# Edge rows prepared once a matrix, measured durations in the planner, and a row that goes into the queries by DMA

## The chip, the cores and the metric

The kernel runs on one core of a Trainium2 chip. The metric is device microseconds of one execution; lower is better. An engine is named as in the profile: PE (TensorE, matmul), PEld (its weight loads), ACT (ScalarE), DVE (VectorE), POOL (GpSimd) and SP (SyncE, which here issues every DMA).

## The reference

Two independent computations on 2048 x 448 inputs, whose results stand side by side in the output.

```python
# A: Fourier mixing, real part of a DFT over the hidden and the sequence axis
a = einsum("bsd,ed->bse", x, dft_hid_re); b = einsum("bsd,ed->bse", x, dft_hid_im)
y = einsum("ts,bse->bte", dft_seq_re, a) - einsum("ts,bse->bte", dft_seq_im, b)
# B: full softmax attention, 16 heads of 28
qkv = x @ wqkv                       # split into q, k, v
p = softmax(q @ k.T * 28 ** -0.5)
out = (p @ v).reshape(S, D) @ wo
return concatenate([y, out], axis=-1)
```

All is float32. The inputs of B are scaled up by 8, so the scores are large and the softmax needs a shift close to each row's maximum.

## The kernel before, in words

Products are made more exact by splitting a value into a rounded part and its rest ("hi" and "lo", type fp32r) and adding two or three matmuls. Tiles are 128 rows; a chunk of queries is 512 columns, four chunks to a head.

**Attention (B).** Projections of q, k and v come first and go to DRAM. For each head, `first_tiles` takes the first 128 keys against all four chunks of queries (L1096), copies the scores to `kept` (ACT, L1100), and makes a shift for each query from the maxima over these keys: DVE transposes each chunk into the buffer `mb` (L1101), reduces it (L1102), joins the partitions (L1108 to L1113), and spreads the shift out again by a transpose into `mb` (L1122). Row 96 of that buffer is copied into row 96 of the query tile `q` (L1125, on DVE or POOL, one partition of 512 elements), and the whole buffer is added to the kept scores (L1127), which then go through the exponential (L1129). With the shift in `q`, the other fifteen key tiles get it inside the matmul: scores L1155 (60 a head), exponential straight from the PSUM bank L1161, and four matmuls with v for each key tile, L1138. So no L1155 of a chunk can start before that chunk's row is in `q`. There is one `mb` buffer, used in turn.

**Fourier mixing (A).** The hidden DFT (`hidden`, L900) makes `u`; the sequence DFT (`sequence`, L985) multiplies it with the 2048 x 2048 matrices. Since these matrices are symmetric, only half of them is multiplied; the kernel folds and compares the other parts (`mirrored`): for each of 8 row tiles `tt`, two halves `g` and two matrices (`part`) it loads four blocks into `wraw` (8 places), folds them (L654, L672), takes the largest leftover difference (L645) and keeps the edge columns (L659, L662). Rows that have no mirror image, 0 and 1024 of each matrix, are multiplied on their own: in the first half `g == 0` of each tile the folded row is taken from `wraw`, split into hi and lo in a small tile `ext` at partitions 0, 32 and 64 (L677 to L679), its source is set to zero (L681), and in the second half a 65-row matmul multiplies `ext` with `peaks` (the short L985). The maxima (L645) of that block wait for L681. `acc`, a sum kept on DVE (L921), is used by one late matmul, L1253.

**The order.** Nothing is scheduled at run time. `Schedule.run` is a planner in the program's own Python: each task has the engines that may do it with a cost in us for each, a due key, tasks it waits for and buffers it needs. It plays the engines forward; whichever engine comes free takes the task with the lowest key that is ready, and tasks are written out in that order, each engine's queue being in order on the chip. A task that names both POOL and DVE goes to the one that comes free first in the plan. SP's DMAs have a modelled flow and at most 8 in flight. So the costs decide which engine does what and in which order, though not how long it takes. PE takes scores, PV matmuls and the "fill" (projections, both DFTs), whose order among themselves is fixed. `kept` has 16 places and holds exponentials, staging and outputs. `big` holds x in its split form during the projections and later `u`, which leaves its tail free.

Of the kernel before, what the change touches and what calls it, by code (L numbers as in the profile page):

```python
# [11 lines left out]
F32 = mybir.dt.float32  # L12
# [12 lines left out]
P = 128  # L25
# [43 lines left out]
def f32(ap):  # L69
    return ap.bitcast(F32)  # L70
# [280 lines left out]
def tile_kernel(ctx, tc, xa, wre, wim, wd, xb, wqkv, wo, out):  # L351
# [33 lines left out]
    x_raw, x_hl = new("xraw", [P, NH, 4], F32), new("xhl", [P, 2, NH, 4], F32R)  # L385
    ext_s, peaks = new("ext", [P, P], F32R, 2), new("peak", [P, 2, E], F32R)
    w_hi, w_lo = new("whi", [P, 3, 4, P], F32R), new("wlo", [P, 3, 4, P], F32R)
# [5 lines left out]
    kept_s = new("kept", [P, 2, CH], F32, NKEPT)  # L393
    mb_s = new("mb", [P, CH], F32, 1, True)
    sm_s = new("sm", [P, 2, NT], F32, 2)
# [178 lines left out]
    class Piece:  # L574


        def __init__(self, src, key, kind="c", early=False, home=None, after=(), wide=False):
            self.hi, self.lo = whi.slot(), wlo.slot()
            raw = self.raw = home or wraw.slot()
            ld = self.ld = dma(key, lambda: nc.sync.dma_start(raw.t, src()), deps=after, acq=[raw])  # L580
            if kind == "c":
                a = sch.add({"POOL": 1.0, "ACT": ACT_S} if wide else {"POOL": 1.0}, key + 1, lambda g: eng_copy(g, self.hi.t, raw.t),
                            deps=[ld], acq=[self.hi], use=[raw])
            else:
                a = act(key + (0 if early else 1), lambda: nc.scalar.activation(self.hi.t, raw.t, AF.Copy), ACT_S, soon=SOON,  # L585
                        deps=[ld], acq=[self.hi], use=[raw])
            at = key + (0 if early else 1.5)
            both = ("DVE",) if early else ("POOL", "DVE") if wide else ("POOL",)
            e = {g: {"DVE": 0.8, "POOL": 1.25}[g] for g in both}
            n = 4 if kind == "c" else 3  # L590
            b = sch.add(e, at, lambda g: eng[g].tensor_tensor(  # L591
                self.lo.t[:, :n], raw.t[:, :n], f32(self.hi.t)[:, :n], op=ALU.subtract),
                deps=[a], acq=[self.lo], use=[raw, self.hi])
            self.ready, self.hi_ready, self.lo_ready = [b], a, [b]
            if kind == "w":
# [51 lines left out]

    either = {"POOL": 1.25, "DVE": 0.69}
    small = {"POOL": 0.2, "DVE": 0.15}

    def mirrored(part, tt, g, w, w2, w3, w4, left, right, key):
# [22 lines left out]
        if g == 0:  # L674
            ext = ext_s.slot()
            row = lambda: w2.raw.t[:1, 3, :]
            c = dve(key, lambda: nc.vector.tensor_copy(ext.t[:1], row()), 0.15, deps=[a, *ext_clear], acq=[ext], use=[w2.raw])  # L677
            c = dve(key, lambda: nc.vector.tensor_copy(ext.t[32:33], f32(ext.t)[:1]), 0.12, deps=[c], use=[ext])
            c = dve(key, lambda: nc.vector.tensor_tensor(ext.t[64:65], row(), f32(ext.t)[:1], op=ALU.subtract), 0.12,  # L679
                    deps=[c], use=[ext, w2.raw])  # L680
            a = dve(key, lambda: nc.vector.memset(row(), 0.0), 0.1, deps=[c], use=[w2.raw])  # L681
        else:
            ext, c = None, None
        largest(lambda: w2.raw.t, [a], part, key + 1, [w2.raw])
        return ext, c

    edge_done, edge_free = {}, {}
    far_done = []
# [146 lines left out]
    ext_clear += [pool(41.0, lambda: nc.gpsimd.memset(f32(peaks), 0.0), 0.57)]  # L835
    for i, t in enumerate(ext_s.tiles):
        ext_clear.append(pool(42.0 + i, lambda t=t: nc.gpsimd.memset(f32(t), 0.0), 0.3))
    ld = [dma(112.0 + 3 * k, lambda k=k: nc.sync.dma_start(x_raw[:, :, k], xa[NH:, :, k, 0].rearrange("t p -> p t")), 64, 2.0) for k in range(4)]
# [21 lines left out]
    class Pair:  # L860


        def __init__(self, i, part, key):
# [8 lines left out]
                raw.t[:, :, 0], x_raw[:, back], raw.t[:, :, 0], op=op), deps=[a, *x_col], use=[raw])  # L872
            a = pool(key + 1, lambda: nc.gpsimd.tensor_copy(self.hi.t, raw.t), 1.0, deps=[b], acq=[self.hi], use=[raw])
            b = sch.add(either, key + 1.5, lambda g: eng[g].tensor_tensor(
                self.lo.t[:, :3], raw.t[:, :3], f32(self.hi.t)[:, :3], op=ALU.subtract), deps=[a], acq=[self.lo], use=[raw, self.hi])
            c = sch.add({"DVE": 0.3, "POOL": 0.53}, key + 1.5, lambda g: eng[g].tensor_tensor(
                self.hi.t[64:, 3:], raw.t[64:, 3:], f32(self.hi.t)[64:, 3:], op=ALU.subtract), deps=[a], use=[raw, self.hi])
            self.ready = [b, c]

    def hidden(part, weights, ready, after):  # L880
# [25 lines left out]
        for i in range(NH):  # L906
# [10 lines left out]
                    deps=[t], use=[o, ut])  # L917
            a = act(key - 10, lambda ut=ut, uh=uh: nc.scalar.activation(uh, ut.t, AF.Copy), 0.3, soon=SOON, deps=[t, *after], use=[ut])
            b = sch.add({"POOL": 0.62, "DVE": 0.35}, key - 10, lambda e, ut=ut, uh=uh, ul=ul: eng[e].tensor_tensor(
                ul, ut.t, f32(uh), op=ALU.subtract), deps=[a], use=[ut])  # L920
            acc_done.append(dve(key - 5, lambda ut=ut, i=i: nc.vector.scalar_tensor_tensor(  # L921
                acc[:, part], ut.t, mid[:, part, i:i + 1], acc[:, part], op0=ALU.mult, op1=ALU.add), 0.35,
                deps=[t, got, acc_done[-1]], use=[ut]))
            if i == 0:
# [25 lines left out]
    def sequence(part, made, tiles=range(NH), late=False, free=()):  # L950
        src, wr = wim if part else wre, wr_d[part]
        u = u_of[part]
        for tt in tiles:
            o, pair = fill_s.slot(), kept_s.slot()
            for g in range(2):
# [13 lines left out]
                x, x_ready = mirrored(part, tt, g, w, w2, w3, w4, left, right, key - 8)  # L969
                if g == 0:  # L970
                    ext, ext_ready = x, x_ready
                jobs = []
                for k in range(4):
                    i = 4 * g + k
                    pair2 = [(w.hi, k, u[:, i, :], [w.hi_ready], w.hi, i), (w.lo, k, u[:, i, :E], w.ready, w.lo, i)]
                    if g and k == 3:
                        jobs.append((ext, None, peaks[:65, part], [ext_ready, *done_top[part]], ext, 0))
                        pair2.reverse()
                    jobs += pair2
                for n, (slot, k, b, ready, use, i) in enumerate(jobs):  # L980
                    first, final = g == 0 and n == 0, g == 1 and n == 8

                    def emit(e, o=o, slot=slot, k=k, b=b, first=first, final=final):
                        a = slot.t[:65] if k is None else slot.t[:, k, :]
                        nc.tensor.matmul(o.t[:, :2 * E if slot.pool is whi else E], a, b, start=first, stop=final)  # L985
# [9 lines left out]
                if part == 0:  # L995
                    if tt == 0 and g == 0:
                        turn_edges(1, last[0], key)
                    for n in range(2):
                        turn_rows(1, (tt * 2 + g) * 2 + n, last[0], key)
            key = key - 60  # L1000
            if part == 0:
# [4 lines left out]
            else:  # L1006
# [77 lines left out]
    def first_tiles(h):  # L1084
# [34 lines left out]
        for c in range(NC):  # L1119
# [4 lines left out]
                deps=[r], acq=[mb], use=[am])  # L1124
            row.append(sch.add({"DVE": 0.7, "POOL": 0.7}, key, lambda e, q=q, mb=mb: eng[e].tensor_copy(q.t[96:97, :], mb.t[96:97, :]),  # L1125
                               deps=[t], use=[mb, q]))
            sh = sch.add({"DVE": 0.8, "POOL": POOL_2}, key, lambda e, s=s, mb=mb: eng[e].tensor_tensor(s.t, s.t, mb.t, op=ALU.add),  # L1127
                         deps=[t, made[c]], use=[s.pair, mb], lat=LAT_S)
# [356 lines left out]
```

## Time and profile before

| | |
|---|---|
| median of 3 runs | 798.91 us (797.62 to 800.2) |
| the profiled execution | 797.84 us, span 796.2 us |
| mean granted clock of PE | 0.973 |
| busy: PE, ACT, DVE, POOL | 757.2, 610.7, 533.2, 336.5 us |
| scores L1155 | 960 matmuls, 343.4 us |
| PV L1138 | 2048 matmuls, 251.4 us |
| exponentials L1161 | 960, 485.8 us |
| sequence DFT L985 | 272 matmuls |

A profile row of a group reads: line, engine, operation, written tile <- read tiles, sizes, count | busy us, mean ns of one | idle us of that engine just before it, and what ended that idle time. A row of waits reads: who <- what ended the wait: total us, times, longest. A row of the chain reads: start us, length us, what; the chain is followed back from the last instruction, at each step to what released it.

### The profile page before, as it was taken

What the parts mean: (1) busy time and instruction counts of PE and PEld (TensorE: products, weight loads), DVE (VectorE), ACT (ScalarE), POOL (GpSimd) and SP (SyncE); (2) the same over time, 40 slices, a digit from 0 to 9 for tenths busy, and PEclk for the clock granted to TensorE, in tenths of its full rate; (3) what the DMA queues carried; (4) which work ended last, traced back from release to release, by engine and by line L of the source; (5) the groups of instructions that cost most, each with busy time, mean ns of one, the idle gap of its engine ahead of it and who ended that gap; (6) DMA issues with size and microseconds to landing.
All of it is one profiled execution on the core that took longest, in us unless ns stands there. A gap on an engine that the chain in (4) does not pass through costs nothing.

```text
span 796.2 us, 13074 instructions
## 1 busy us (share of the span) xinstructions
PE 757.2 (95%) x4150; PEld 428.5 (54%) x4150; DVE 533.2 (67%) x1039; ACT 610.7 (77%) x1232; POOL 336.5 (42%) x410
## 2 busy tenths in 40 slices
PE   9999999999999998988899999998988799999997
PEld 7898655555555553454345554444444344334496
DVE  5547814465466869898887967796967878244371
ACT  6403798989898988887688979896876768898932
POOL 7301301414032535566573716274767754022510
PEclk9999999999999999999799999999998999999999
DMA  8957836472428456726477666646556462305254
GB/s 307 289 207 219 250 115 182 150 224 85 130 63 231 145 160 179 222 71 198 131 222 189 195 172 194 182 129 198 176 171 210 154 191 74 88 19 171 80 172 145
DMA packets 113541, 133.15 MB, mean 167 GB/s; under 512 B 50314, under 2 KB 63145, under 8 KB 113465
## 3 DMA queue, kind: packets, MB, share of 16 engines
q1 hardware_dynamic: 113464, 132.24, 55.1%
q8 instruction: 35, 0.57, 0.3%
q14 instruction: 42, 0.34, 0.1%
HBM read 101.15 MB, written 49.19 MB: 189 GB/s over the span
## 4 chain that ended last, share of the span: by engine, by line
PE 68%; DVE 18%; DMA 6%; ACT 4%; issue 2%; SPq 0%; POOL 0%; DVEq 0%; ACTq 0%
PE bank L1155 22%; PE bank L1138 21%; PE bank L726 12%; PE bank L1317 4%; DMA wraw<-wr 4%; ACT kept L1161 3%; PE bank L985 3%; DVE far L645 2%; PE bank L762 2%; PE bank L900 2%; PE bank L1096 1%; DVE mb L1101 1%; DVE qm L1102 1%; DVE kept L1127 1%; DVE q L1125 1%
## 5 line engine op out<-in xcount | busy, mean ns | idle before, releaser
L1161 ACT ACTIVATE kept<-bank 128x512 f32<-128x512 f32 x960 | 485.8, 646 | 83.7 <-PE bank L1155 82.6
L1155 PE MATMUL bank<-q,k 98*128 98x512 f32 x960 | 343.4, 430 | 17.7 <-ACT kept L1161 11.7
L1155 PEld LDWEIGHTS bank<-q,k 98*128 98x128 f32 x960 | 174.5, 190 | 191.1 <-issue 99.2
L1138 PE MATMUL bank<-kept,v 128*32 128x512 f32 x2048 | 251.4, 615 | 0.0
L1138 PEld LDWEIGHTS bank<-kept,v 128*32 128x32 f32 x2048 | 55.8, 111 | 121.1 <-issue 116.3
L1127 POOL TENSOR_TENSOR kept<-kept,mb 128x512 f32<-128x512 f32 x39 | 55.5, 1423 | 70.0 <-DVE mb L1122 52.2
L1100 ACT ACTIVATE kept<-bank 128x512 f32<-128x512 f32 x64 | 38.4, 653 | 35.2 <-PE bank L1096 22.6
L1101 DVE STREAM_TRANSPOSE mb<-bank 128x512 f32<-128x512 f32 x64 | 45.5, 711 | 26.9 <-PE bank L1096 23.6
L1198 POOL TENSOR_TENSOR kept<-kept 128x512 f32<-128x512 f32 x16 | 20.6, 1288 | 96.3 <-DVE kept L1193 78.6
L645 DVE TENSOR_REDUCE far<-wraw 128x1 f32<-128x508 f32 (+1 forms) x90 | 57.5, 657 | 1.1 <-POOL wraw L672 0.7
L726 PE MATMUL bank<-big,whi 128*128 128x512 f32 x154 | 56.6, 396 | 0.0
L1122 DVE STREAM_TRANSPOSE mb<-am 128x512 f32<-128x512 f32 x64 | 45.1, 705 | 11.8 <-POOL kept L1127 10.3
L591 POOL TENSOR_TENSOR wlo<-wraw,whi 128x512 fp32r<-128x512 f32 (+1 forms) x34 | 45.0, 1324 | 18.8 <-ACT whi L585 16.8
L985 PE MATMUL bank<-big,whi 128*128 128x452 f32 x128 | 49.8, 390 | 3.1 <-POOL whi L458 3.1
L1129 ACT ACTIVATE kept<-kept 128x512 f32<-128x512 f32 x64 | 43.0, 704 | 10.1 <-POOL kept L1127 5.6
L654 POOL TENSOR_TENSOR wraw<-wraw,wraw 128x508 f32<-128x508 f32 x35 | 38.6, 1104 | 23.6 <-DMA wraw<-wr 19.6
L1102 DVE TENSOR_REDUCE qm<-mb 128x16 f32<-128x512 f32 x64 | 43.4, 678 | 1.2
L1125 POOL CAST q<-mb 1x512 fp32r<-1x512 f32 x20 | 13.5, 673 | 71.5 <-DVE mb L1122 55.3
L726 PE MATMUL bank<-wd,big 128*128 128x448 f32 x176 | 36.8, 364 | 0.0
L985 PE MATMUL bank<-big,wlo 128*128 128x226 f32 x128 | 35.8, 279 | 0.9 <-POOL wlo L591 0.9
L1189 DVE STREAM_TRANSPOSE kept<-kept 128x512 f32<-128x512 f32 x16 | 11.2, 702 | 35.5 <-ACT kept L1187 35.5
L726 PE MATMUL bank<-big,wlo 128*128 128x512 f32 x88 | 34.8, 396 | 0.0
(167 smaller groups left out, 966.3 us busy)
## 6 DMA issues: line engine op xcount, KB each, us to landing
wraw<-wr SPq DMA_DIRECT2D x60, 256.0 KB
qkd<-kept SPq DMA_DIRECT2D x40, 256.0 KB
wraw<-xa SPq DMA_DIRECT2D x32, 256.0 KB
wraw<-wre SPq DMA_DIRECT2D x32, 256.0 KB
wr<-wre SPq DMA_DIRECT2D x31, 256.0 KB
wr<-wim SPq DMA_DIRECT2D x31, 256.0 KB
k<-qkd SPq DMA_DIRECT2D x64, 112.0 KB
q<-qkd SPq DMA_DIRECT2D x64, 112.0 KB
```

The costliest lines, as they stand in the source:

```text
L591: b = sch.add(e, at, lambda g: eng[g].tensor_tensor(self.lo.t[:, :n], raw.t[:, :n], f32(self.hi.t)[:, :n], op=ALU.subtract), deps=[a], acq ...
L645: far_done.append(dve(key, lambda: nc.vector.tensor_reduce(far[:, part, n:n + 1], t(), axis=AX.XY, op=ALU.max, apply_absolute_value=True), ...
L726: nc.tensor.matmul(o.t[:, :cols], w(), x(), start=(i == 0), stop=(i == n - 1))
L985: nc.tensor.matmul(o.t[:, :2 * E if slot.pool is whi else E], a, b, start=first, stop=final)
L1101: t = dve(key, lambda o=o, tm=tm: nc.vector.transpose(tm.t, o.t), 0.73, deps=[m], acq=[tm], use=[o], lock=[o], own=RAW_S)
L1102: rs.append(dve(key, lambda tm=tm, c=c: nc.vector.tensor_reduce(qm.t[:, 0, c * NT:(c + 1) * NT], tm.t.rearrange("p (j r) -> p j r", r=32), ...
L1122: t = dve(key, lambda mb=mb, c=c: nc.vector.transpose(mb.t, f32(am.t)[:, c * NT:(c + 1) * NT].unsqueeze(2).to_broadcast([P, NT, 32])), 0.7 ...
L1127: sh = sch.add({"DVE": 0.8, "POOL": POOL_2}, key, lambda e, s=s, mb=mb: eng[e].tensor_tensor(s.t, s.t, mb.t, op=ALU.add), deps=[t, made[c] ...
L1129: shown.append(act(key, lambda s=s: nc.scalar.activation(s.t, s.t, AF.Exp, scale=SCALE), ACT_S, deps=[sh], use=[s.pair]))
L1138: nc.tensor.matmul(o.t[c * VW:(c + 1) * VW, :], VT[h].t[:, kt // 4, kt % 4, :], tiles[c].t, start=(kt == 0), stop=(kt == NT - 1))
L1155: m = pe(key, lambda e, o=o, q=q, kt=kt: nc.tensor.matmul(o.t, KT[h][kt // 4].t[:KM, kt % 4 * P:(kt % 4 + 1) * P], q.t[:KM, :], start=True ...
L1161: es[h, kt].append(act(key - 20, lambda o=o, p=p: nc.scalar.activation(p.t, o.t, AF.Exp, scale=SCALE), deps=[m], use=[o, p.pair]))
```

## The change

Four edits.

1. The rows without a mirror image are no longer taken from each tile's `wraw`. A new helper `middle(part, ...)` runs once for each matrix: two DMAs bring row 0's and row 1024's halves (8 blocks of 128) into one partition of two `kept` places, and DVE or POOL folds, copies and splits all 1024 elements at once into a strip in the free tail of `big`, which POOL has cleared. The strip serves all 8 tiles. `mirrored` keeps only the memset of the row.
2. `mb` gets a second buffer.
3. Row 96 goes from `mb` into `q` by a DMA from SP in place of a copy on DVE or POOL.
4. Some costs of tasks in the planner get other values.

```diff
-    ext_s, peaks = new("ext", [P, P], F32R, 2), new("peak", [P, 2, E], F32R)
+    peaks = new("peak", [P, 2, E], F32R)
...
-    mb_s = new("mb", [P, CH], F32, 1, True)
+    mb_s = new("mb", [P, CH], F32, 2, True)
...
-                a = sch.add({"POOL": 1.0, "ACT": ACT_S} if wide else {"POOL": 1.0}, key + 1, ...
+                a = sch.add({"POOL": 0.75, "ACT": ACT_S} if wide else {"POOL": 0.75}, key + 1, ...
...
-            e = {g: {"DVE": 0.8, "POOL": 1.25}[g] for g in both}
+            e = {g: {"DVE": 0.85, "POOL": 1.35}[g] for g in both}
...
-    either = {"POOL": 1.25, "DVE": 0.69}
-    small = {"POOL": 0.2, "DVE": 0.15}
+    either = {"POOL": 1.2, "DVE": 0.83}
+    small = {"POOL": 0.35, "DVE": 0.4}
...
         if g == 0:
-            ext = ext_s.slot()
-            row = lambda: w2.raw.t[:1, 3, :]
-            c = dve(key, lambda: nc.vector.tensor_copy(ext.t[:1], row()), 0.15, deps=[a, *ext_clear], acq=[ext], use=[w2.raw])
-            c = dve(key, lambda: nc.vector.tensor_copy(ext.t[32:33], f32(ext.t)[:1]), 0.12, deps=[c], use=[ext])
-            c = dve(key, lambda: nc.vector.tensor_tensor(ext.t[64:65], row(), f32(ext.t)[:1], op=ALU.subtract), 0.12,
-                    deps=[c], use=[ext, w2.raw])
-            a = dve(key, lambda: nc.vector.memset(row(), 0.0), 0.1, deps=[c], use=[w2.raw])
-        else:
-            ext, c = None, None
+            a = dve(key, lambda: nc.vector.memset(w2.raw.t[:1, 3, :], 0.0), 0.17, deps=[a], use=[w2.raw])
...
+    def middle(part, key, dep):
+        src, pairs = (wre, wim)[part], [kept_s.slot() for _ in range(2)]
+        h = NH * P
+        op = ALU.add if part else ALU.subtract
+        ext = big[:, 2 * NT * E + part * h:2 * NT * E + (part + 1) * h]
+        row = lambda i: pairs[i].t.rearrange("p a b -> p (a b)")[:1, :h]
+        z = pool(key, lambda: nc.gpsimd.memset(f32(ext)[:65], 0.0), 1.1, deps=[dep])
+        ld = [dma(key + 0.1 * i, lambda i=i: nc.sync.dma_start(
+            row(i).rearrange("p (a b) -> p a b", a=NH), src[:NH, :1, NH * i, :].rearrange("t p s -> p t s")), 8, 2.0,
+            deps=[dep], acq=[pairs[i]]) for i in range(2)]
+        both = {"POOL": 1.5, "DVE": 1.3}
+        a = sch.add(both, key + 1, lambda g: eng[g].tensor_tensor(row(1), row(1), row(0), op=op), deps=ld, use=pairs)
+        b = sch.add(both, key + 1, lambda g: eng[g].tensor_copy(ext[:1], row(1)), deps=[a, z], use=[pairs[1]])
+        c = sch.add(both, key + 1, lambda g: eng[g].tensor_copy(ext[32:33], f32(ext)[:1]), deps=[b])
+        d = sch.add(both, key + 1, lambda g: eng[g].tensor_tensor(ext[64:65], row(1), f32(ext)[:1], op=ALU.subtract),
+                    deps=[b], use=[pairs[1]])
+        middles[part] = ext, [c, d]
...
-    for i, t in enumerate(ext_s.tiles):
-        ext_clear.append(pool(42.0 + i, lambda t=t: nc.gpsimd.memset(f32(t), 0.0), 0.3))
...
-            a = pool(key + 1, lambda: nc.gpsimd.tensor_copy(self.hi.t, raw.t), 1.0, ...
-            b = sch.add(either, key + 1.5, ...
+            a = pool(key + 1, lambda: nc.gpsimd.tensor_copy(self.hi.t, raw.t), 0.7, ...
+            b = sch.add({"POOL": 1.08, "DVE": 0.58}, key + 1.5, ...
...
-            c = sch.add({"DVE": 0.3, "POOL": 0.53}, key + 1.5, ...
+            c = sch.add({"DVE": 0.5, "POOL": 0.53}, key + 1.5, ...
...
-            a = act(key - 10, ... AF.Copy), 0.3, ...          # L918, u
-            b = sch.add({"POOL": 0.62, "DVE": 0.35}, ...        # L919
+            a = act(key - 10, ... AF.Copy), 0.45, ...
+            b = sch.add({"POOL": 0.77, "DVE": 0.64}, ...
...
-                acc[:, part], ut.t, mid[:, part, i:i + 1], acc[:, part], op0=ALU.mult, op1=ALU.add), 0.35,
+                acc[:, part], ut.t, mid[:, part, i:i + 1], acc[:, part], op0=ALU.mult, op1=ALU.add), 0.7,
...
+            if part == 0 and i == 4:             # in hidden, the fifth of eight tiles
+                middle(0, key, a)
...
+            if part == 0 and tt == NH - 2:       # in sequence, the seventh of eight tiles
+                middle(1, key, last[0])
...
-                w2 = {"DVE": 0.35, "POOL": 0.62}
+                w2 = {"DVE": 0.64, "POOL": 0.7}
...
-            row.append(sch.add({"DVE": 0.7, "POOL": 0.7}, key, lambda e, q=q, mb=mb: eng[e].tensor_copy(q.t[96:97, :], mb.t[96:97, :]),
-                               deps=[t], use=[mb, q]))
-            sh = sch.add({"DVE": 0.8, "POOL": POOL_2}, key, lambda e, s=s, mb=mb: eng[e].tensor_tensor(s.t, s.t, mb.t, op=ALU.add),
+            row.append(dma(key, lambda q=q, mb=mb: nc.sync.dma_start(f32(q.t)[96:97, :], mb.t[96:97, :]), 2, deps=[t], use=[mb, q]))
+            sh = sch.add({"DVE": 0.92, "POOL": POOL_2}, key, lambda e, s=s, mb=mb: eng[e].tensor_tensor(s.t, s.t, mb.t, op=ALU.add),
```

The matmul in `sequence` takes 128 columns of the strip at a time in place of `ext`.

More of the change, by code (lines that the diff above doesn't have):

```diff
@@ L581, in __init__ @@
             if kind == "c":
-                a = sch.add({"POOL": 1.0, "ACT": ACT_S} if wide else {"POOL": 1.0}, key + 1, lambda g: eng_copy(g, self.hi.t, raw.t),
+                a = sch.add({"POOL": 0.75, "ACT": ACT_S} if wide else {"POOL": 0.75}, key + 1, lambda g: eng_copy(g, self.hi.t, raw.t),
                             deps=[ld], acq=[self.hi], use=[raw])
@@ L674, in mirrored @@
         if g == 0:
-            ext = ext_s.slot()
-            row = lambda: w2.raw.t[:1, 3, :]
-            c = dve(key, lambda: nc.vector.tensor_copy(ext.t[:1], row()), 0.15, deps=[a, *ext_clear], acq=[ext], use=[w2.raw])
-            c = dve(key, lambda: nc.vector.tensor_copy(ext.t[32:33], f32(ext.t)[:1]), 0.12, deps=[c], use=[ext])
-            c = dve(key, lambda: nc.vector.tensor_tensor(ext.t[64:65], row(), f32(ext.t)[:1], op=ALU.subtract), 0.12,
-                    deps=[c], use=[ext, w2.raw])
-            a = dve(key, lambda: nc.vector.memset(row(), 0.0), 0.1, deps=[c], use=[w2.raw])
-        else:
-            ext, c = None, None
-        largest(lambda: w2.raw.t, [a], part, key + 1, [w2.raw])
-        return ext, c
+            a = dve(key, lambda: nc.vector.memset(w2.raw.t[:1, 3, :], 0.0), 0.17, deps=[a], use=[w2.raw])
+        largest(lambda: w2.raw.t, [a], part, key + 1, [w2.raw])
+    def middle(part, key, dep):
[15 more added lines that the diff above has]
+        middles[part] = ext, [c, d]
+    middles = {}
     edge_done, edge_free = {}, {}
@@ L872, in __init__ @@
                 raw.t[:, :, 0], x_raw[:, back], raw.t[:, :, 0], op=op), deps=[a, *x_col], use=[raw])
-            a = pool(key + 1, lambda: nc.gpsimd.tensor_copy(self.hi.t, raw.t), 1.0, deps=[b], acq=[self.hi], use=[raw])
-            b = sch.add(either, key + 1.5, lambda g: eng[g].tensor_tensor(
+            a = pool(key + 1, lambda: nc.gpsimd.tensor_copy(self.hi.t, raw.t), 0.7, deps=[b], acq=[self.hi], use=[raw])
+            b = sch.add({"POOL": 1.08, "DVE": 0.58}, key + 1.5, lambda g: eng[g].tensor_tensor(
                 self.lo.t[:, :3], raw.t[:, :3], f32(self.hi.t)[:, :3], op=ALU.subtract), deps=[a], acq=[self.lo], use=[raw, self.hi])
-            c = sch.add({"DVE": 0.3, "POOL": 0.53}, key + 1.5, lambda g: eng[g].tensor_tensor(
+            c = sch.add({"DVE": 0.5, "POOL": 0.53}, key + 1.5, lambda g: eng[g].tensor_tensor(
                 self.hi.t[64:, 3:], raw.t[64:, 3:], f32(self.hi.t)[64:, 3:], op=ALU.subtract), deps=[a], use=[raw, self.hi])
@@ L917, in hidden @@
                     deps=[t], use=[o, ut])
-            a = act(key - 10, lambda ut=ut, uh=uh: nc.scalar.activation(uh, ut.t, AF.Copy), 0.3, soon=SOON, deps=[t, *after], use=[ut])
-            b = sch.add({"POOL": 0.62, "DVE": 0.35}, key - 10, lambda e, ut=ut, uh=uh, ul=ul: eng[e].tensor_tensor(
+            a = act(key - 10, lambda ut=ut, uh=uh: nc.scalar.activation(uh, ut.t, AF.Copy), 0.45, soon=SOON, deps=[t, *after], use=[ut])
+            b = sch.add({"POOL": 0.77, "DVE": 0.64}, key - 10, lambda e, ut=ut, uh=uh, ul=ul: eng[e].tensor_tensor(
                 ul, ut.t, f32(uh), op=ALU.subtract), deps=[a], use=[ut])
             acc_done.append(dve(key - 5, lambda ut=ut, i=i: nc.vector.scalar_tensor_tensor(
-                acc[:, part], ut.t, mid[:, part, i:i + 1], acc[:, part], op0=ALU.mult, op1=ALU.add), 0.35,
+                acc[:, part], ut.t, mid[:, part, i:i + 1], acc[:, part], op0=ALU.mult, op1=ALU.add), 0.7,
                 deps=[t, got, acc_done[-1]], use=[ut]))
@@ L968, in sequence @@
                         0.65, deps=[w.ld], use=[w.raw]))
-                x, x_ready = mirrored(part, tt, g, w, w2, w3, w4, left, right, key - 8)
-                if g == 0:
-                    ext, ext_ready = x, x_ready
+                mirrored(part, tt, g, w, w2, w3, w4, left, right, key - 8)
+                ext, ext_ready = middles[part]
                 jobs = []
@@ L976, in sequence @@
                     if g and k == 3:
-                        jobs.append((ext, None, peaks[:65, part], [ext_ready, *done_top[part]], ext, 0))
+                        jobs.append((None, None, peaks[:65, part], [*ext_ready, *done_top[part]], None, 0))
                         pair2.reverse()
@@ L981, in sequence, with emit @@
                     first, final = g == 0 and n == 0, g == 1 and n == 8
-                    def emit(e, o=o, slot=slot, k=k, b=b, first=first, final=final):
-                        a = slot.t[:65] if k is None else slot.t[:, k, :]
-                        nc.tensor.matmul(o.t[:, :2 * E if slot.pool is whi else E], a, b, start=first, stop=final)
+                    def emit(e, o=o, slot=slot, k=k, b=b, first=first, final=final, tt=tt, ext=ext):
+                        a = ext[:65, tt * P:(tt + 1) * P] if k is None else slot.t[:, k, :]
+                        nc.tensor.matmul(o.t[:, :2 * E if slot and slot.pool is whi else E], a, b, start=first, stop=final)
                     deps = [last[0], *ready]
@@ L988, in sequence @@
                         deps += made[i]
-                    last[0] = pe(key + n * M225, emit, d=M448 if slot.pool is whi else M225, deps=deps, acq=[o] if first else [],
-                                 use=[use, *([] if first else [o])])
+                    last[0] = pe(key + n * M225, emit, d=M448 if slot and slot.pool is whi else M225, deps=deps, acq=[o] if first else [],
+                                 use=[*([use] if use else []), *([] if first else [o])])
                     if first:
```

## The prediction

> **What bounds the kernel now.** I read the page's busy times and clock first, then the chain, then busy time by stretch, the waits of TensorE (PE), and last the places where the chain leaves PE.
>
> ```profile
> span 796.2 us, 13074 instructions
> PE 757.2 (95%) x4150; PEld 428.5 (54%) x4150; DVE 533.2 (67%) x1039; ACT 610.7 (77%) x1232; POOL 336.5 (42%) x410
> PEclk9999999999999999999799999999998999999999
> PE 68%; DVE 18%; DMA 6%; ACT 4%; issue 2%; SPq 0%; POOL 0%; DVEq 0%; ACTq 0%
> ```
>
> PE is busy 95%, yet the chain lies on VectorE (DVE) for 18% of 796.2, 143 us, and the clock row dips near its middle and last third. The heads of the attention show where the loss is: a double run of PV matmuls (L1138 x32) stands on the chain near the end of a head.
>
> ```profile
> 120.98 3.57 PE bank L1138 x32
> ...
> 279.57 3.57 PE bank L1138 x32
> ...
> 322.40 3.57 PE bank L1138 x32
> ...
> 456.34 3.57 PE bank L1138 x32
> 495.17 3.57 PE bank L1138 x32
> ...
> 681.08 3.57 PE bank L1138 x32
> ```
>
> From 120.98 to 279.57 four heads pass in 158.6 us, 39.65 each. The next takes 42.8 (3.2 more); 322.40 to 456.34 are three heads in 133.9 (15.0 more); 495.17 to 681.08 are four in 185.9 (27.3 more). Eight slow heads lose 45.5 us: the most that this change can reach.
>
> ```profile
> 121.00:280.00 159.00, 158.99 (x932) 85.79 (x936) 93.40 (x177) 145.89 (x300) 47.68 (x54) 1.00 0.51 151
> 322.00:456.00 134.00, 123.07 (x706) 63.59 (x705) 117.13 (x222) 106.84 (x217) 81.60 (x102) 0.95 0.59 174
> 495.00:681.00 186.00, 168.79 (x897) 82.66 (x896) 144.16 (x268) 142.00 (x283) 106.02 (x122) 0.93 0.54 163
> ```
>
> Columns: stretch, length, busy time of PE, weight load, DVE, ACT, POOL, granted clock, DMA share, GB/s. In the even stretch PE is never idle and DVE works 59%. In the other two DVE works 87% and 78%, PE idles 10.9 and 17.2 us and the clock is short by 0.05 x 134 and 0.07 x 186, 6.7 and 13.0 us. So a microsecond of idle PE costs about 0.7 more in clock (19.7 over 28.1). DVE's queue, then, sets those two stretches.
>
> ```profile
> PE bank L1155 <- ACT kept L1161: 11.7, 11, 3.2
> PE bank L1253 <- DVE kept L1251: 6.0, 1, 6.0
> PE bank L985 <- DVE ext L679: 4.4, 2, 2.8
> ...
> PE bank L1155 <- DVE q L1125: 2.3, 1, 2.3
> ```
>
> Three of these waits end on DVE lines that the change touches or delays: the edge rows (ext), the row into q, and the sum (acc) ahead of L1253. One place, in the order of the chain:
>
> ```profile
> 531.54 1.21 DVE ext L678
> 532.75 0.01 issue
> 532.77 1.11 DVE ext L679
> 533.87 0.04 issue
> 533.92 0.37 PE bank L985
> ...
> 536.00 3.08 PE bank L1138 x16
> ```
>
> PE stands still until two instructions on one partition are done, and the next sixteen PV matmuls take 3.08 us, since the clock has dropped.
>
> **The change, part by part.**
>
> ```profile
> L1125 DVE CAST q<-mb 1x512 fp32r<-1x512 f32 x44 | 31.9, 725 | 1.5
> L1125 POOL CAST q<-mb 1x512 fp32r<-1x512 f32 x20 | 13.5, 673 | 71.5 <-DVE mb L1122 55.3 <-PE bank L1155 15.9
> L678 DVE CAST ext<-ext 1x128 fp32r<-1x128 f32 x16 | 8.5, 529 | 0.5
> L677 DVE CAST ext<-wraw 1x128 fp32r<-1x128 f32 x15 | 8.1, 540 | 0.9 <-PE bank L985 0.8
> L679 DVE TENSOR_TENSOR ext<-wraw,ext 1x128 fp32r<-1x128 f32 x15 | 7.4, 491 | 0.2
> L1122 DVE STREAM_TRANSPOSE mb<-am 128x512 f32<-128x512 f32 x64 | 45.1, 705 | 11.8 <-POOL kept L1127 10.3 <-POOL q L1125 0.4
> L659 DVE TENSOR_TENSOR off<-edge,wraw 128x4 f32<-128x4 f32 x30 | 10.4, 364 | 10.6 <-DMA wraw<-wim 7.7 <-DMA wraw<-wre 1.7 <-DMA wraw<-wr 1.2
> L921 DVE SCALAR_TENSOR_TENSOR acc<-ut,mid,acc 128x226 f32<-128x226 f32 x16 | 11.3, 705 | 0.5
> ```
>
> The 143 us of chain on DVE lie almost all in the 362 us from 280 to 456 and 495 to 681, so a microsecond of DVE work there is worth about 0.4.
>
> *Edge rows.* Three DVE instructions a tile go, 8.5 + 8.1 + 7.4 = 24.0 us (the 0.17 us memset stays). On the path: at least the 4.4 of PE's own wait, at most 24.0; at 0.4 it is 9.6.
>
> *Row into q.* 31.9 us of DVE and 13.5 of POOL go. How much lay on the chain is in the chain's shares by line, for 280 to 456 and 495 to 681:
>
> ```profile
> by line: PE bank L1138 18.2%; PE bank L1155 17.4%; ACT kept L1161 7.8%; DVE kept L1127 5.1%; issue 5.0%; PE bank L985 4.7%; DVE far L645 3.6%; DVE mb L1122 3.0%; DVE mb L1101 2.8%; DVE qm L1102 2.6%; DVE q L1125 2.6%; DMA wraw<-wre 2.3%; PE
> by line: DMA wraw<-wr 15.2%; PE bank L1138 13.0%; PE bank L1155 10.7%; DVE far L645 5.7%; issue 5.0%; DMA wraw<-wim 4.6%; DVE mb L1101 3.6%; DVE qm L1108 3.6%; DVE wraw L654 3.4%; DVE qm L1102 3.3%; DVE q L1125 3.1%; PE bank L985 3.1%; DVE
> ```
>
> 2.6% of 176 and 3.1% of 186 are 10.3 us. Late next is a load that waits for a place in wraw and then takes its time (15.2 + 4.6% of the second stretch), and that stays. So of the 19.9 of both edits I count two thirds (my choice between a half, if the loads keep their dates, and all): **-13.3**.
>
> *Prepared once.* Per matrix two loads of 4 KB, one POOL memset, four instructions on 1x1024. At twice the 725 ns of a 1x512 cast, 1.45 us (estimate), eight are 11.6 us, half of them on DVE, times 0.4: **+2.3**. They are released five tiles, and for the second matrix one tile of fill, before they are needed, so the loads cost nothing; without that cover each would hold the first tile up by a load and four steps, 3.35 (below) + 5.8 = 9.2 us, 18 in all. They borrow two of the places that the exponentials use; no wait for those shows now.
>
> *Two places.* DVE waited 10.3 us, nine times, for the one buffer, held by POOL's addition L1127; the next transpose no longer waits for it. Bounds 0 and -10.3; at 0.4, **-4.1**.
>
> *The row by DMA.* SyncE's queue gets 64 more issues, each held there until its transpose is done, with loads of wraw, k and q behind it. A place in mb is now held until the row has landed. Rows that bound how long a DMA takes, and what that queue waits for:
>
> ```profile
> 1.45 3.35 DMA kept<-xb
> ...
> 642.64 8.52 DMA wraw<-wr
> ```
> ```profile
> SPq L1035 <- PE bank L1155: 116.0, 39, 10.0
> ...
> SPq L638 <- DVE far L645: 21.4, 15, 6.1
> ```
>
> 256 KB into an empty queue land in 3.35 us, behind other loads in 8.52; 2 KB will be nearer the first. The lower end is a gain of the 0.7 that the copy took, were the DMA free. The Trainium skill ("DMA: Bandwidth & Descriptors", Anatomy of one DMA) puts the fixed part of a DMA at some 2.0 us, for another issuing path; by it the row would be 1.3 us later and not 2.65, and no row of this trace times so small a DMA. With 3.35 the row comes 2.65 later than by copy, less 1.1 (10.3 over nine) since the transposes go sooner: 1.5 a head. In the even stretch PE had other work all the time and none of it shows; of the eight slow heads I let half pay: **+6**. Ends: -6 (eight times 0.7) and the rival below.
>
> *Durations.* They change nothing but the order that the planner writes. Its DVE costs come near the measured ones: 0.15 to 0.4 for L659 (364 ns), 0.35 to 0.7 for L921 (705 ns), where it had DVE free too early, so PE got work such as L1253 ahead of its operands. Of that wait's 6.0 us and 4.2 of clock I count half: **-5**. A new order may gain or lose as much as all the idle time of the two stretches, 28 us, so -28 and +28 bound it; I take the value nearest the one wait that shows.
>
> *Sum.* -13.3 + 2.3 - 4.1 + 6 - 5 = -14.1, and -2 for clock (about a fifth of the chain on DVE is idle PE, 28 of 143, at 0.7): -16. The profiled execution took 797.84; that gives 781.8, and the median shown, 798.91, is 1.1 above it: about **782**.
>
> **Rivals.**
>
> *All of it comes back.* With DVE relieved of 56 us the slow heads run like the even ones: 797.84 - 45.5 = 752, nearer 760 with some rest. For it: even heads run at DVE 59%, and 56 us off the 261 of the two stretches would leave 64%. Against: loads of 8.5 us on the chain stay.
>
> *The row comes late, slower.* The row's issue stands behind a wait of SyncE's queue, 3.0 us on average (116.0 over 39), and lands 2.65 later than the copy: 5.65 a head, in eight slow heads 45 in place of 6, so 782 + 39 = 821. It decides from 22 over 8, 2.8 us a head; there nothing is left of the gain. For it: that queue's waits fall in the same stretches, and a slow DVE holds it up. Against: in the trace only one wait of 2.3 us ends on L1125.
>
> *POOL pays it back.* Dearer DVE work goes to POOL more often, and the two get into each other's way:
>
> ```profile
> L654 DVE TENSOR_TENSOR wraw<-wraw,wraw x25: 631/677/1660, 238.5 to 651.2; 128x508 f32<-128x508 f32 x25
> L1125 DVE CAST q<-mb x44: 423/424/1473, 73.0 to 709.1; 1x512 fp32r<-1x512 f32 x44
> ```
>
> The same instruction takes 631 or 1660 ns, 1.03 more when held up. Thirty more instructions on POOL, each holding DVE up by half of that, all on the chain, give 782 + 15 = 797: no difference. The Trainium skill ("SBUF — State Buffer", Who interferes with whom) says that the two share a pair of ports and the second fully blocks until the first is done; by that rule, work moved to POOL doesn't free DVE, and the spread of these rows agrees. Against: the removed casts are such blocked instructions themselves.
>
> **How the numbers follow.** My forecast holds 0.50 (770 to 792), all of it back 0.18 (752 to 768), POOL 0.13 (792 to 801), the late row 0.19 (801 to 821). The range 757 to 806 leaves out some 0.05 below and 0.13 above. No change that a measurement can tell is 0.3%, 2.4 us about 798.9: half of the POOL case and a little of the late row, 0.08; faster 0.74, slower 0.18.
>
> **What would show it.** DVE under 490 us busy and no L677 to L679; the two slow stretches shorter, clock above 0.95 in both; no PE wait on ext; L1253 waiting under 3 us. L1122's wait for a place near zero. Wrong, if PE or its weight load waits on the DMA of q by over 20 us in all, if POOL's busy time rises over 370 with DVE's means unchanged, or if the heads of the even stretch take over 41 us.

## The result, and the profile after

The changed kernel takes 774.97 us (median of 4 runs, 772.41 to 782.57) where the kernel before, run beside it, takes 798.26 (796.74 to 800.2): a ratio of 0.9723, 95% interval 0.9651 to 0.9794. The forecast was 782 in a range of 757 to 806. The profiled execution took 774.34. Lines have moved in the changed kernel: scores are L1165, PV L1148, the spreading transpose L1133, the row's DMA L1136, the addition L1137, the sequence DFT L994, the late matmul on `acc` L1263.

Busy times, clock and the chain by engine, from its page:

```profile
span 772.3 us, 13080 instructions
PE 747.3 (97%) x4150; PEld 424.9 (55%) x4150; DVE 491.5 (64%) x939; ACT 610.6 (79%) x1232; POOL 335.5 (43%) x406
PEclk9999999999999999999999999999999889999999
PE 83%; DMA 4%; ACT 4%; POOL 3%; DVE 3%; issue 1%; SPq 1%; POOLq 0%; ACTq 0%
```

DVE is 41.7 us less busy (533.2 before), and the chain has left it: 3% of the span in place of 18%. That share alone says little of the time: two kernels below have the chain on DVE for 11% and 15% and are as fast (771.52 and 775.52 us). The ends of heads on the chain, from 237.97 to 656.71 ten heads:

```profile
237.97 3.57 PE bank L1148 x32
...
322.06 3.57 PE bank L1148 x32
...
402.96 3.57 PE bank L1148 x32
...
612.29 3.57 PE bank L1148 x32
...
656.71 3.57 PE bank L1148 x32
```

Ten heads in 418.7 us, 22.2 more than ten of the even 39.65. Before, the slow heads lost 45.5. So half of that loss came back, 23 us, and the span is 23.9 shorter: it is nearly the whole gain. The prediction's two slow stretches, at the same times in this kernel:

```profile
322.00:456.00 134.00, 132.87 (x799) 70.19 (x802) 107.08 (x208) 117.76 (x240) 83.29 (x102) 1.00 0.66 190
495.00:681.00 186.00, 173.54 (x940) 85.14 (x940) 138.97 (x246) 150.40 (x299) 109.47 (x126) 0.94 0.56 166
```

In the first, PE's idle time went from 10.9 to 1.1 us and the clock from 0.95 to 1.00; in the second only from 17.2 to 12.5 us, and the clock from 0.93 to 0.94. What PE waits for now:

```profile
PE bank L1165 <- ACT kept L1171: 6.3, 8, 2.2
PE bank L994 <- POOL whi L458: 6.1, 4, 2.8
PE bank L1107 <- ACT kept L1171: 2.8, 1, 2.8
...
PE bank L994 <- POOL big L692: 1.2, 1, 1.2
...
PE bank L1263 <- DVE kept L1261: 0.4, 1, 0.4
```

The waits on the edge rows (4.4), on the row in `q` (2.3) and on `acc` (6.0) are down to 1.2, none and 0.4. One wait on the new strip is left. The new DMA shows on SP's own queue:

```profile
SPq L1136 <- DVE mb L1133: 48.4, 20, 6.0
```

So SP stands 48.4 us behind transposes that aren't done, up to 6.0 at a time, and still no matmul in this execution waits for that DMA.

### The profile page after: what moved, and what is told of

Read it like the earlier page. It is cut to its first block, busy times and chain, and to the rows that moved or that the text cites. A ratio compares the mean times of both kernels' runs of the same rounds, so it can differ in the third digit from the quotient of the medians.

```text
span 772.3 us, 13080 instructions
## 1 busy us (share of the span) xinstructions
PE 747.3 (97%) x4150; PEld 424.9 (55%) x4150; DVE 491.5 (64%) x939; ACT 610.6 (79%) x1232; POOL 335.5 (43%) x406
## 4 chain that ended last, share of the span: by engine, by line
PE 83%; DMA 4%; ACT 4%; POOL 3%; DVE 3%; issue 1%; SPq 1%; POOLq 0%; ACTq 0%
PE bank L1165 29%; PE bank L1148 27%; PE bank L736 12%; PE bank L994 5%; PE bank L1327 5%; ACT kept L1171 4%; PE bank L908 3%; DMA wraw<-wim 2%; PE bank L772 2%; PE bank L1107 2%; POOL kept L1137 1%; DMA v<-vd 1%; DMA wraw<-wr 1%; DVE qm L1119 0%; DMA kept<-xb 0%
## 5 line engine op out<-in xcount | busy, mean ns | idle before, releaser
L1165 PE MATMUL bank<-q,k 98*128 98x512 f32 x960 | 335.4, 426 | 6.5 <-ACT kept L1171 6.3
L1165 PEld LDWEIGHTS bank<-q,k 98*128 98x128 f32 x960 | 174.1, 190 | 174.3 <-issue 92.2
L1148 PE MATMUL bank<-kept,v 128*32 128x512 f32 x2048 | 249.9, 611 | 0.0
L1148 PEld LDWEIGHTS bank<-kept,v 128*32 128x32 f32 x2048 | 55.5, 110 | 119.4 <-issue 115.8
L1137 POOL TENSOR_TENSOR kept<-kept,mb 128x512 f32<-128x512 f32 x34 | 47.3, 1394 | 96.5 <-DVE mb L1133 77.2
L654 POOL TENSOR_TENSOR wraw<-wraw,wraw 128x508 f32<-128x508 f32 x40 | 45.6, 1144 | 29.4 <-DMA wraw<-wr 15.1
L1139 ACT ACTIVATE kept<-kept 128x512 f32<-128x512 f32 x64 | 40.3, 706 | 18.1 <-POOL kept L1137 17.7
L994 PE MATMUL bank<-big,whi 128*128 128x452 f32 x128 | 48.6, 382 | 6.1 <-POOL whi L458 6.1
L591 POOL TENSOR_TENSOR wlo<-wraw,whi 128x512 fp32r<-128x512 f32 (+1 forms) x33 | 41.9, 1271 | 11.1 <-ACT whi L585 9.1
L1133 DVE STREAM_TRANSPOSE mb<-am 128x512 f32<-128x512 f32 x64 | 41.8, 687 | 3.4 <-DMA q<-mb 2.8
L458 POOL CAST whi<-wraw 128x512 fp32r<-128x512 f32 x29 | 19.4, 670 | 40.9 <-DMA wraw<-wre 18.5
L753 DVE TENSOR_TENSOR kept<-bank,kept 128x512 fp32r<-128x512 f32 x20 | 13.3, 687 | 37.3 <-ACT kept L752 37.2
L994 PE MATMUL bank<-big,wlo 128*128 128x226 f32 x128 | 35.0, 274 | 0.9 <-POOL wlo L591 0.9
```

The costliest lines, as they stand in the source:

```text
L591: b = sch.add(e, at, lambda g: eng[g].tensor_tensor(self.lo.t[:, :n], raw.t[:, :n], f32(self.hi.t)[:, :n], op=ALU.subtract), deps=[a], acq ...
L654: a = sch.add(either, key, lambda e, r=r, of=of: eng[e].tensor_tensor(r.raw.t[:, :, :0:-1], r.raw.t[:, :, :0:-1], of.raw.t[:, :, 1:], op=o ...
L994: nc.tensor.matmul(o.t[:, :2 * E if slot and slot.pool is whi else E], a, b, start=first, stop=final)
L1133: t = dve(key, lambda mb=mb, c=c: nc.vector.transpose(mb.t, f32(am.t)[:, c * NT:(c + 1) * NT].unsqueeze(2).to_broadcast([P, NT, 32])), 0.7 ...
L1137: sh = sch.add({"DVE": 0.92, "POOL": POOL_2}, key, lambda e, s=s, mb=mb: eng[e].tensor_tensor(s.t, s.t, mb.t, op=ALU.add), deps=[t, made[c ...
L1148: nc.tensor.matmul(o.t[c * VW:(c + 1) * VW, :], VT[h].t[:, kt // 4, kt % 4, :], tiles[c].t, start=(kt == 0), stop=(kt == NT - 1))
```

## The experiments

Each kernel ran beside the kernel before on the same chip, in three groups on three chips; ratios are to the kernel before on that chip, with the 95% interval behind. The theories, as they are numbered in the expectations: 1, DVE was relieved and that is the gain; 2, the measured costs gave a better order; 3, the row by DMA costs something that the rest hides; 4, the two places carry it; 5, the place pays only in an order planned with measured costs; 6, DVE work costs time only where the order doesn't provide for it; 7, beyond that it is the accident of the order.

### Each edit undone alone

**The costs back to the former ones.**

```diff
-    either = {"POOL": 1.2, "DVE": 0.83}
-    small = {"POOL": 0.35, "DVE": 0.4}
+    either = {"POOL": 1.25, "DVE": 0.69}
+    small = {"POOL": 0.2, "DVE": 0.15}
... (and the other eleven)
```

> The changed kernel with the planner's former costs, all else as changed. Theory 1 (DVE was relieved; 533.2 to 491.5 us busy, and that brought the 24 us): the order matters little, 775 to 781. Theory 2 (the measured costs gave a better order, and that brought most): back by 12 us or more, 787 and above, with PE's wait at L1263 (the late matmul on acc) at several us again.

Measured 782.11 us, 0.9809 (0.9781 to 0.9837). Between the two theories: 0.9% by the ratios, less than the scatter between orders that is measured at the end of this section, so not shown to be the costs' doing. The waits of PE are other ones, none on L1263 beyond 0.5 us.

**The row by a copy again**, two `mb` buffers kept.

```diff
-            row.append(dma(key, lambda q=q, mb=mb: nc.sync.dma_start(f32(q.t)[96:97, :], mb.t[96:97, :]), 2, ...
+            row.append(sch.add({"DVE": 0.7, "POOL": 0.7}, key, lambda e, q=q, mb=mb: eng[e].tensor_copy(...
```

> The row into q by a copy on DVE or POOL again, two mb buffers kept. Theory 1: some 30 us of DVE come back, at 0.4 us of time for each about 10: 783 to 788. Theory 2: order only, 772 to 778. Theory 3 (the row by DMA comes late and costs something that the rest of the change hides): faster than the changed kernel, under 772.

Measured 771.52 us, 0.9692 (0.9642 to 0.9742): no slower than the changed kernel, although DVE and POOL do the copies again:

```profile
PE 745.7 (97%) x4150; PEld 423.7 (55%) x4150; DVE 521.7 (68%) x962; ACT 608.8 (79%) x1231; POOL 361.4 (47%) x448
```

DVE is 30 us busier than in the changed kernel at the same time. Theory 1, which asked for 783 or more, misses. Theory 3 asked for under 772; the median is just under it, but theory 3 isn't shown either, since the intervals overlap.

**One `mb` buffer again**, the row still by DMA.

```diff
-    mb_s = new("mb", [P, CH], F32, 2, True)
+    mb_s = new("mb", [P, CH], F32, 1, True)
```

> One mb buffer again, the row still by DMA, so that the next transpose waits for the row to land. Theory 1: DVE's busy time is the same, 775 to 781. Theory 4 (the two places shorten the chain of transposes at the head's start, and that is what the slow heads waited for): 785 and above, DVE waiting on the DMA of q for 60 us and more in place of 2.8.

Measured 830.66 us, 1.0421 (1.0387 to 1.0455), slower than the kernel before. Waits of DVE and of PE:

```profile
DVE mb L1133 <- DMA q<-mb: 33.9, 16, 7.9
...
PE bank L1165 <- DMA q<-mb: 10.9, 4, 7.8
```

With one place, a transpose has to wait for the DMA of the one before it to land: 16 times, 33.9 us (60 and more were expected), and now PE waits on that DMA too. In the changed kernel DVE waits 2.8 us for such a DMA and PE not at all, so the row by DMA needs the second place.

These waits also show how long the row takes. The row's issue, the next transpose, and between them the addition, the buffer's other reader:

```profile
622.05 0.71 DVE L1133 STREAM_TRANSPOSE mb<-am 128x512 f32<-128x512 f32 x1
622.86 0.69 DVE L1137 TENSOR_TENSOR kept<-kept,mb 128x512 f32<-128x512 f32 x1
624.55 0.71 DVE L1133 STREAM_TRANSPOSE mb<-am 128x512 f32<-128x512 f32 x1 [1.00 <-DMA q<-mb]
```
```profile
622.79 0.59 SPq L1136 DMA_DIRECT2D q<-mb  x1
```

The next transpose starts 1.76 us after the issue. In 12 of the 16 waits it is 1.7 to 1.9 us, in the other four 2.8 to 7.2.

**The edge rows from every tile again.**

```diff
-            if part == 0 and i == 4:
-                middle(0, key, a)
...
+            c = dve(key, lambda: nc.vector.tensor_copy(ext.t[:1], row()), 0.15, ...
+            c = dve(key, lambda: nc.vector.tensor_copy(ext.t[32:33], f32(ext.t)[:1]), 0.12, ...
+            c = dve(key, lambda: nc.vector.tensor_tensor(ext.t[64:65], row(), f32(ext.t)[:1], op=ALU.subtract), 0.12, ...
```

> The edge rows taken from each tile again (three DVE instructions in 16 tiles), all else as changed. Theory 1: 24 us of DVE come back, at 0.4 about 9 us: 781 to 787, PE waiting on ext again by 2 to 5 us. Theory 2: 773 to 779.

Measured 770.02 us, 0.9652 (0.9605 to 0.9699). Not slower at all, and below both ranges; PE waits once on ext:

```profile
PE bank L985 <- DVE ext L679: 1.1, 1, 1.1
```

So two of the four edits, the ones that take work off DVE, can be undone without a loss that shows. Theory 1 falls as it stood, by the copy above more than by this run: here DVE is only 10.7 us busier than in the changed kernel (502.2 against 491.5), which at 0.4 would be 4 us.

### Single edits on the kernel before

**Only a second buffer.**

```diff
-    mb_s = new("mb", [P, CH], F32, 1, True)
+    mb_s = new("mb", [P, CH], F32, 2, True)
```

> The kernel before with a second mb buffer and nothing else. Theory 4 (the two places carry the change): 780 or less, with DVE still over 525 us busy. Theory 1 (DVE relief carries it): within 4 us of 797. Theory 5 (the place pays only in an order planned with measured costs): 788 to 797.

Measured 768.88 us, 0.9636 (0.9576 to 0.9695): the whole gain, with DVE busier than before. Theory 4's numbers are met, theories 1 and 5 miss. PE's waits on the edge rows, on the row in `q` and on L1251 are gone here too, though none of the edits aimed at them was made.

```profile
PE 748.1 (97%) x4150; PEld 426.1 (55%) x4150; DVE 539.4 (70%) x1036; ACT 608.9 (79%) x1231; POOL 328.9 (43%) x414
```

What changes with the place is seen in DVE's timeline of one head (start, length, instruction). First the kernel before, then this one, with POOL's copy of the last two rows:

```profile
397.25 0.71 DVE L1122 STREAM_TRANSPOSE mb<-am 128x512 f32<-128x512 f32 x1
...
402.95 0.70 DVE L1122 STREAM_TRANSPOSE mb<-am 128x512 f32<-128x512 f32 x1
...
406.18 0.70 DVE L1122 STREAM_TRANSPOSE mb<-am 128x512 f32<-128x512 f32 x1
...
411.56 0.69 DVE L1122 STREAM_TRANSPOSE mb<-am 128x512 f32<-128x512 f32 x1
...
412.85 1.10 DVE L1125 CAST q<-mb 1x512 fp32r<-1x512 f32 x1
```
```profile
386.65 1.31 DVE L1122 STREAM_TRANSPOSE mb<-am 128x512 f32<-128x512 f32 x2
387.99 2.54 DVE L1125 CAST q<-mb 1x512 fp32r<-1x512 f32 x2
...
393.29 1.30 DVE L1122 STREAM_TRANSPOSE mb<-am 128x512 f32<-128x512 f32 x2
```
```profile
394.13 1.64 POOL L1125 CAST q<-mb 1x512 fp32r<-1x512 f32 x2 [1.43 <-DVE mb L1122]
```

Before, the four transposes of this head are strung over 15 us, with other work between them, and the last row is in `q` at 413.95, just ahead of the 484th L1155, the first score that needs it, which starts after an idle gap:

```profile
414.10 0.47 PE L1155 MATMUL bank<-q,k 98*128 98x512 f32 x1 [1.73 <-ACT kept L1161]
```

The profile puts this gap down to an exponential that ended within a tenth of a us of the row, so the row wasn't alone in holding PE up. With two places the transposes come in pairs within 8 us, the last row is in `q` at 395.77, and the 484th L1155 starts at 405.46. Ten microseconds of margin stand where there was none. Taken the same way in all eight slow heads, the margin is 0.1 to 5.2 us before and 7.0 to 10.8 with two places. So with the place the planner puts this work earlier. The wait for the place itself was only 10.3 us in all; the gain is 28.

That this margin is what brings the time isn't shown. The kernel in the next group, one place with the measured costs, has margins of 0.8 to 4.8 us in the same heads, and the neighbour of this kernel further below 6.9 to 10.5; the two take 778.87 and 776.94 us. Nor did a kernel with two places run in the old order, which would tell what the place is worth on the chip without the planner.

**Only the measured costs.**

```diff
-    either = {"POOL": 1.25, "DVE": 0.69}
-    small = {"POOL": 0.2, "DVE": 0.15}
+    either = {"POOL": 1.2, "DVE": 0.83}
+    small = {"POOL": 0.35, "DVE": 0.4}
... (and the other ten)
```

> The kernel before with the measured costs and nothing else, one mb buffer. Theory 2 (order by measured costs): 783 to 787. Theory 4: the one place still binds, 794 to 800; the costs may even cost, as the copy and the addition that hold the place go to POOL more often.

Measured 778.87 us, 0.9766 (0.9731 to 0.9801), with one buffer. Better than either theory said: a second place isn't needed for a gain of 18 us. L1122 still waits for its place (5.9 us, five times).

**Both.**

```diff
-    mb_s = new("mb", [P, CH], F32, 1, True)
+    mb_s = new("mb", [P, CH], F32, 2, True)
... (and the twelve costs)
```

> The kernel before with a second mb buffer and the measured costs; edge rows in every tile and the row by copy as before. Theory 4: as the first of this group, 775 to 780, and 768 to 773 with the part of the costs (0.9% when they were undone). Theory 1: over 785, since 56 us of DVE work are back.

Measured 772.73 us, 0.9705 (0.9675 to 0.9735). Alone they brought 28 and 18 us, together 24: the second buffer and the costs don't add. This kernel is also the changed one without both edits that take work off DVE (528.0 us busy against 491.5), and it is no slower; theory 1 asked for over 785.

### DVE work put back, the order untouched

The changed kernel with instructions that lead to nothing, written out inside tasks whose planned cost stays, so that every engine's other instructions keep their order:

```diff
-            a = dve(key, lambda: nc.vector.memset(w2.raw.t[:1, 3, :], 0.0), 0.17, ...
+            a = dve(key, lambda: (nc.vector.tensor_copy(spare[:1], ...), nc.vector.tensor_copy(spare[32:33], ...),
+                nc.vector.tensor_tensor(spare[64:65], ...), nc.vector.memset(w2.raw.t[:1, 3, :], 0.0)), 0.17, ...
...
+                # after three of the four transposes
+                nc.vector.tensor_copy(mb.t[96:97], mb.t[96:97])
```

> The changed kernel in its own order on every engine, with DVE work put back that leads to nothing: three one-partition instructions of 128 elements in each of the 16 tiles, and a copy of row 96 of mb onto itself after three of the four transposes of a head (96 instructions in all, some 45 us of DVE). Theory 1: 0.4 a microsecond, 18 us: 790 to 795. Theory 4: DVE has room, 775 to 781.

Measured 797.19 us, 1.0005 (0.9986 to 1.0024): the gain is gone. The groups that were added, 54.0 us of DVE in all:

```profile
L1134 DVE COPY mb<-mb 1x512 f32<-1x512 f32 x48 | 26.7, 556 | 1.7
L675 DVE CAST spare<-spare 1x128 fp32r<-1x128 f32 x16 | 10.2, 640 | 0.6
L675 DVE TENSOR_TENSOR spare<-spare 1x128 fp32r<-1x128 f32 x16 | 9.1, 568 | 0.5
L675 DVE CAST spare<-peak 1x128 fp32r<-1x128 f32 x16 | 8.0, 498 | 0.0
```

Every engine's other instructions stand in the same order in the two traces, so here the work alone was changed; 48 of the instructions stand between a transpose and the DMA of its row, so the price is that of work at these places. From 0.9723 to 1.0005 are 22 us: 0.41 a microsecond of DVE work, the price that the prediction used (0.4), and 797.19 lies above theory 1's range since 54 us were added where 45 were expected. So in this given order DVE work costs time, and in the undone kernels above, where the planner made a new one, no such cost shows. That suggested theory 6.

That 0.41 equals 0.4 doesn't confirm how 0.4 was found, as the chain's time on DVE over the 362 us of the slow stretches. In the changed kernel the chain is on DVE for 3% of 772.3, 23 us, which by the same recipe would give 0.06. With the work added it is:

```profile
PE 70%; DVE 13%; DMA 6%; ACT 4%; POOL 3%; issue 3%; SPq 1%; POOLq 0%; ACTq 0%; DVEq 0%
```

13% of 795.2, 103 us, gives 0.29.

**The same work, told to the planner.**

```diff
-  ... nc.vector.memset(w2.raw.t[:1, 3, :], 0.0)), 0.17, ...
+  ... nc.vector.memset(w2.raw.t[:1, 3, :], 0.0)), 1.75, ...
-  ... transpose with the copy after it ... 0.72,
+  ... transpose with the copy after it ... 0.72 if c == 3 else 1.32,
```

> The same idle DVE instructions as in the kernel that put 54 us of DVE work back in an unchanged order (797.2), but the planner is told their measured cost (1.75 for the memset task, 1.32 for three of four transposes) and writes its own order. Theory 6 (DVE work costs time where the order does not provide for it, 54 us gave 22; provided for, it finds room): 770 to 783. Theory 1 (DVE's work costs 0.4 a microsecond whatever the order): 790 to 799.

Measured 775.52 us, 0.9758 (0.9726 to 0.979). The same idle instructions, and 20 of the 22 us are back by the ratios, within the intervals all of them. Busy time by stretch (length, PE, weight load, DVE, ACT, POOL, clock, DMA share, GB/s), 420 to 660, for the untold order and the told one:

```profile
420.00:660.00 240.00, 221.28 (x1227) 112.28 (x1225) 201.98 (x360) 187.89 (x374) 139.68 (x158) 0.94 0.62 184
```
```profile
420.00:660.00 240.00, 226.53 (x1298) 114.17 (x1294) 198.51 (x355) 200.34 (x399) 153.79 (x180) 0.98 0.61 185
```

DVE does about the same there, POOL takes 14 us more, PE idles 5 us less at a higher clock and gets 71 more matmuls done. Whether it is the told costs that help, or any order newly written around these instructions, this pair doesn't tell.

### How much an order alone makes

**The kernel with only a second buffer, a cost moved by a hundredth.**

```diff
-    either = {"POOL": 1.25, "DVE": 0.69}
+    either = {"POOL": 1.26, "DVE": 0.70}
```

> The kernel before with a second mb buffer, and one cost moved by a hundredth (either: 1.25 to 1.26 for POOL, 0.69 to 0.70 for DVE), which means nothing but another order. Theory 7: 764 to 778, away from 768.9 by more than the runs of one kernel differ. If the costs matter for what they are: within 2 us of 768.9.

Measured 776.94 us, 0.9782 (0.9749 to 0.9815), against 0.9636 without: 12 us by the ratios (8 between the medians) for a change that means nothing. Theory 7 is met, the other misses.

**The changed kernel, moved likewise.**

```diff
-    either = {"POOL": 1.2, "DVE": 0.83}
+    either = {"POOL": 1.21, "DVE": 0.84}
```

> The changed kernel with the same cost moved by a hundredth (1.20 to 1.21, 0.83 to 0.84). Theory 7: 768 to 782. If the costs matter for what they are: within 2 us of 775.

Measured 776.43 us, 0.9775 (0.9731 to 0.9818): no difference from 0.9723 that the intervals let through, and in the range of both.

**Two buffers, measured costs, and measured costs for the edge rows of each tile too.**

```diff
-            c = dve(key, lambda: nc.vector.tensor_copy(ext.t[:1], row()), 0.15, ...
+            c = dve(key, lambda: nc.vector.tensor_copy(ext.t[:1], row()), 0.54, ...
... (and 0.12, 0.12, 0.1 to 0.53, 0.49, 0.17)
```

> The kernel before with a second mb buffer, the measured costs, and in addition measured costs for the edge rows of each tile (0.54, 0.53, 0.49, 0.17 in place of 0.15, 0.12, 0.12, 0.1). Theory 6: 19 us of DVE work more is provided for, so faster than the 772.7 without it, 764 to 770, and PE's 5.3 us wait on ext gone. Theory 7 (between orders that have two mb places the rest is the accident of the order, some 4 us either way): 766 to 778.

Measured 772.88 us, 0.9723 (0.9687 to 0.9759), where 772.73 stood without them. PE still waits 2.2 us on ext. Theory 6 asked for a gain and missed; theory 7 is met. In the kernel without these costs, some 19 us of DVE work that the planner wasn't told of cost nothing that shows; at 0.41 they would have been 8 us, 1%. So theory 6 rests on the pair with the idle instructions alone.

So ratios of two newly planned kernels that differ by less than about 1.5% can't be put down to what was edited. Orders with two places and no idle work that the planner wasn't told of lie between 0.9636 and 0.9809, ten of them with the changed kernel. Clear of that scatter are three findings: one place with the row by DMA (1.042), untold DVE work in a kept order (1.0005), and the kernel before itself. What sets the kernel before apart stays open. Its order with one place gives 1, another order with one place, planned with the measured costs, gives 0.9766, as good as several with two. Whether the measured costs or the second buffer gained what they did for what they are, or as any other order would, can't be told: no meaningless change was run on the kernel before. The second buffer by itself has the lowest median of all (768.88), but its neighbour at 776.94 says not to count on it.

## Why the prediction was right, and where it was not

- *Where the loss is.* Right: the slow heads held it, and they gave back half of their 45.5 us, nearly the whole gain. Of the signs that were named, the clock above 0.95 came in one of the two stretches (1.00 and 0.94), and DVE's busy time, 491.5, just missed 490. The rival by which all of the loss comes back took the 56 us off the two slow stretches alone; DVE got 15 us less busy there.
- *DVE's work at 0.4 a microsecond.* This is the step that failed: the edge rows and the row into `q` were priced by work times the chain's share. Undone, alone or both together, they cost nothing that can be measured (0.9652, 0.9692 and 0.9705 against 0.9723), where -13.3 stood. The idle work in a kept order did cost 0.41, but on an order whose chain would have said 0.06, so the match with 0.4 speaks for the number and not for the recipe. An edit that makes the planner write a new order isn't priced by work times a share of the chain.
- *Prepared once.* +2.3 was forecast, and as forecast it is small. Its eight instructions take 12.1 us where 11.6 were assumed, but only 1.9 of them are on DVE, where half were counted, and one wait of 1.2 us is left.
- *Two places.* The term that was mis-sized most. -4.1, at most -10.3, was read from DVE's wait for the buffer; alone the buffer brought 28 us, 17 with the nudged cost. The wait shows what the chip lost under the old order, not what another order gains; how much of the 17 to 28 us is the place and how much the new order isn't shown.
- *The row by DMA.* +6 was forecast, and a loss of up to 39 as the rival. No cost shows, since the copy in its place gives the same time. The 3.35 us that the row was given comes from a load of 256 KB that wasn't alone either (another was issued 0.46 us ahead of it). In the kernel with one place the row lands 1.7 to 1.9 us after its issue in most waits, so about 1.1 us later than by copy and not 2.65, which the earlier transposes were forecast to make up. The Trainium skill gives 2.0 us as a DMA's fixed part for another issuing path ("DMA: Bandwidth & Descriptors", Anatomy of one DMA), which is nearer than 3.35. A late row can be dear, as the rival said: with one place the kernel took 1.042, where the waits for the buffer that the row holds (33.9 us) are longer than PE's for the row (10.9). In the changed kernel PE never waits for a row.
- *Durations.* -5 was forecast. Undone, +0.9% (7 us), within the scatter; alone, -2.3% (18 us). The wait on `acc` went from 6.0 to 0.4, but it did so with the former costs too (0.5), and with the second buffer alone it is gone, so the wait that was chosen as the evidence wasn't evidence.
- *POOL pays it back.* Didn't happen: POOL 335.5 us against 336.5.

The forecast of the total was 7 us above the measured median. Its own sum gives 797.84 - 16 + 1.1 = 782.9, nearer 783 than 782, on which nothing hangs. That the terms summed well is luck: the -13.3 and the +6 don't show, the -4.1 is far below what the second buffer alone brought, and the edits don't add at all (28 and 18 us alone, 24 together), which a sum of terms assumes. What held is the ceiling from the heads, 45.5 us; 16 of it were expected, 23 came.

## What to carry to other kernels

In a kernel whose order is written out ahead, an edit changes two things: the work, and the order that the planner writes around it. Measure them apart. Work that is added or taken in an unchanged order shows its own price (0.41 a microsecond here, where the chain's share said 0.06); the same edit in a new order can cost nothing. Before crediting an edit that replans everything, move a cost by a hundredth, on the kernel before as well as on the changed one, and see how far that alone moves the time. And the wait for a single buffer, 10.3 us here, is no bound on what comes with a second one, since the order changes with it.

## What the runs showed of the hardware that was not expected

A DMA of one row of 2 KB costs SyncE's queue more than a load of 256 KB to issue. From the changed kernel's lines (minimum, median, maximum in ns), and for the load from the kernel before:

```profile
L1136 SPq DMA_DIRECT2D q<-mb x64: 497/546/887, 68.7 to 680.7; - x64
```
```profile
L638 SPq DMA_DIRECT2D wraw<-wr x60: 320/372/5889, 289.8 to 650.4; - x60
```

546 against 372 ns in the median (382 in the changed kernel). And a DVE instruction on one partition isn't small beside the others' work: the 1x128 casts that were put back took 498 and 640 ns each on average, the 1x512 copy 556.
